# K and Q of the first three pairs of heads, issued by SP and ScalarE instead of SP alone

## The chip, the cores and the metric

One core of one Trainium2 chip. The metric is device time in microseconds (us); the kernel before took 608.39 us in the median of three runs. Engines: TensorE (PE; PEld is its weight load), VectorE (DVE), ScalarE (ACT), GpSimd (POOL) and SyncE (SP), which here only issues transfers.

## What is computed

Attention over 4 sequences of 576 tokens with 8 heads of 64, masked in blocks of 64, then two expert layers on the 2304 tokens. Cut to what matters:

```python
scores = (q @ k.T) / 8                     # per head; masked where block_i < block_j
x = softmax(scores) @ v                    # heads side by side: (2304, 512)
x = maximum(maximum(x @ w1, x @ w2), x @ w3) @ w_out
# then a layer of 8 experts: rows with x @ w_skip > 0 get the arg-max expert of x @ w_gate:
#   x + gate * (relu(x @ w1[e]) @ w2[e])
```

## The kernel before

The tokens are worked in six chunks of 384 (`CH`). For each chunk, attention runs by pairs of heads: a group is one chunk's tokens of one sequence and one pair (`groups`, L564 to L568). Chunk 0 has four groups, one for each pair, all of sequence 0. A group has units of up to 128 queries (`units`, L593 to L596); each of the first four groups has three, with 128, 256 and 384 keys.

`load(i)` (L571 to L582) brings a group's K and Q. The two heads of a pair lie on partitions 0 to 63 and 64 to 127 of the tiles `k` and `q`, and each half is a transfer of its own: K and Q of the first head, then K and Q of the second, four issues on SP, 96 KB each in chunk 0. `load_v` (L584) brings V. `load_ident` (L963) brings the identity that the transposes need. The weights of the first expert layer come as 18 pieces of 512 KB (`raw_words`, L492) and 6 of its second matrix; each is decoded on ScalarE and VectorE (L503 to L534).

A unit of attention is a chain over engines: scores on TensorE (L613, then a mask product at L620), a maximum on VectorE (L637) and its scaling (L651), the exponentials on ScalarE (L662), sums and reciprocals on VectorE (L673, L677), normalizing on either (L683, L685), transposes on TensorE (L697), a copy out (L702), the product with V (L716), and two parts of the result (L726, L724). When all units of a chunk are done, the dense products with the decoded weights (L742) start for it.

`start_masks` (L953) writes the masks on VectorE and runs one small exponential on ScalarE (L961), in front of which ScalarE loads its table.

**The order of the work.** The order on every engine is made when the program is built, by a planner (`Plan`, L60). `build` (L158) makes one `Task` for each step with an engine, a planned duration, a due time `at`, the tasks it depends on and the buffers it takes. `order` (L94) draws tasks one by one: on each engine those that can start within 0.05 planned us of the earliest compete, the lowest due time wins, and of the five engines' winners the earliest start is taken (of equal starts, the engine that comes first in PE, ACT, DVE, POOL, SP). The tasks are then sorted by planned start and emitted, so each engine's queue runs in that order. A task with `nbytes` ends when a planned transfer has ended (one after another, at 230 GB/s) and 2.0 planned us have gone by.

A load of K and Q is a task on SP of 2.5 planned us (L188), the identity one of 0.6 (L182), V one of 0.5 (L193), a weight piece one of 0.6 (L292), the constants one of 1.8 (L287). There are three buffers for Q, six for K, two for V and three for weight pieces (L1026). A Q buffer is free again when all scores of its group are done (L279), so the fourth group's load waits for the first group's scores. Scores depend on their group's load:

```python
deps.append(kq[i])                                                              # L212
sc = S.add("PE", dur, at, lambda ks=ks: [E.sc(k) for k in ks], deps, acq, mode="R")
```

Of the kernel before, what the change touches and what calls it, by code (L numbers as in the profile page):

```python
# [8 lines left out]
F32 = mybir.dt.float32  # L9
# [8 lines left out]
B, H, S, D = 4, 8, 576, 64  # L18
# [3 lines left out]
P = 128  # L22
CH = 384
# [126 lines left out]
def act_time(n, src="psum"):  # L150
    return (0.04 if src == "psum" else 0.09) + 0.83e-3 * n


def dve_time(n, fast=False):
    return 0.07 + (0.52e-3 if fast else 1.045e-3) * n


def build(S, E, groups, units):  # L158
# [4 lines left out]
    def later(name, t, *readers):  # L163
        for r in readers:
            r.releases.append((name, t))

    kq, vv = {}, {}
# [5 lines left out]
    for u in units:  # L173
        c = u[1]
        n = seen.get(c, 0)
# [4 lines left out]
        first_of.setdefault(u[0], k)  # L180
    start = S.add("DVE", 1.0, -1e3, E.masks)
    ident = S.add("SP", 0.6, when[0] - 11.5, E.ident, nbytes=65536)  # L182
    sc_of, pv_of, k_tile = {}, {}, {}
    for i, (c, b, qlo, qhi, tiles, hp) in enumerate(groups):
        at = when[first_of[i]] - 12
        names = ["q"] + (["k"] if qlo == 0 else [])
        n = qhi - qlo
        t = kq[i] = S.add("SP", 2.5, at, lambda i=i: E.load(i), acq=names, nbytes=2 * P * n * 4)  # L188
        if qlo == 0:
            k_tile[b, hp] = t  # L190
        else:
            t.deps.append(k_tile[b, hp])
        vv[i] = S.add("SP", 0.5, at + 1, lambda i=i: E.load_v(i), acq=["v"], nbytes=(qhi + P - 1) // P * P * P * 4)  # L193
# [3 lines left out]
    n = 0  # L197
# [7 lines left out]
    for ks in su:  # L205
        at = when[ks[0]]
        dur, acq, deps = 0.0, [], [start]
        for k in ks:
            i, c, hp, q0, nq, nk, col, first = units[k]
            dur += nk * 4 / 2400 + 0.05  # L210
            acq += ["sc"] * (2 if nk > 512 and nq == P else 1)
            deps.append(kq[i])  # L212
        sc = S.add("PE", dur, at, lambda ks=ks: [E.sc(k) for k in ks], deps, acq, mode="R")
        tps = []
        for n, k in enumerate(ks):
            i, c, hp, q0, nq, nk, col, first = units[k]
            at = when[k]
            nkt = (nk + P - 1) // P
            sets, parts = (1, 2 if nk > 512 else 1) if nq == 64 else (2, 2 if nk > 512 else 1)
            w = nk // parts  # L220
            one = dve_time(w * 2 if sets == 2 else w * parts)
            mk = [S.add("DVE", 0.13, at - 2.2, lambda k=k: E.mk(k), [sc])] if nq == P and c > 1 else []
            mx = S.add("DVE", one * (parts if sets == 2 else 1), at - 2, lambda k=k: E.mx(k), [sc] + mk)
            if parts == 2:
                mx = S.add("DVE", 0.07, at - 2.5, lambda k=k: E.m2(k), [mx])
            mx = S.add("DVE", 0.07, at - 2.5, lambda k=k: E.ms(k), [mx])
            exs = []
            for j in range(sets):
                exs.append(S.add("ACT", parts * (0.24 + 0.83e-3 * w), at - 2 + 0.1 * j, lambda k=k, j=j: E.ex(k, j),
                                 [mx] + exs, ["p"] if j == 0 else []))  # L230
            for _ in range(2 if nk > 512 and nq == P else 1):
                later("sc", sc, *exs)
            rs = S.add("DVE", 0.07, at - 3, lambda k=k: E.ra(k), exs)
            rs = S.add("DVE", 0.08, at - 3, lambda k=k: E.rs(k), [rs])
            nms = []
            for j in range(sets):
                nm = S.add(dict(ACT=0.19 + 0.83e-3 * nk, **(dict(DVE=0.13 + 0.52e-3 * nk) if c != 1 else {})), 0, at - 2.5 + 0.1 * j, None, [rs])
                nm.emit = lambda k=k, j=j, nm=nm: E.nm(k, j, nm.on)
                nms.append(nm)
            todo = sets * nkt  # L240
            evs = []
            for m in range(0, todo, 4):
                z = min(4, todo - m)
                tp = S.add("PE", 0.107 * z, at - 1, lambda k=k, m=m: E.tp(k, m),
                           nms + [ident] + ([tp0] if m else []),
                           ["tp"] + (["pT"] if m == 0 else []), mode="T")
                ev = S.add(dict(ACT=act_time(128 * z), **(dict(DVE=dve_time(128 * z)) if c > 1 else {})), 0, at - 5, None, [tp])
                ev.emit = lambda k=k, m=m, ev=ev: E.ev(k, m, ev.on)
                later("tp", tp, ev)
                later("p", exs[0], tp)  # L250
                if m == 0:
                    tp0 = tp
                evs.append(ev)
            last_pv[k] = (tp0, evs, nkt)
        deps, dur, acq = [], 0.0, []
        for k in ks:
            i, c, hp, q0, nq, nk, col, first = units[k]
            deps += last_pv[k][1] + [vv[i]]
            dur += last_pv[k][2] * (0.213 if nq == P else 0.107)
            acq.append("tp")  # L260
        c = units[ks[0]][1]
        if c not in x_first:
            acq.append("x")
        pv = S.add("PE", dur, when[ks[0]] - 0.5, lambda ks=ks: [E.pv(k) for k in ks], deps, acq, mode="C")
        x_first.setdefault(c, pv)
        if pv is not x_first[c]:
            pv.deps.append(x_first[c])
        for k in ks:
            i, c, hp, q0, nq, nk, col, first = units[k]
            xh = S.add("ACT", act_time(nq), when[k] - 4, lambda k=k: E.xh(k), [pv])  # L270
            xl = S.add("DVE", dve_time(nq), when[k] - 4, lambda k=k: E.xl(k), [xh])
            later("tp", pv, xl)
            later("pT", last_pv[k][0], pv)
            all_x[c] += [xh, xl]
            sc_of.setdefault(units[k][0], []).append(sc)
            pv_of.setdefault(units[k][0], []).append(pv)
# [13 lines left out]
    for k in range(18 + NF):  # L290
        at = first_w + w_pace * k if k < 18 else 16 + 3.0 * (k - 18)
# [22 lines left out]
    for c in range(NCH):  # L314
# [3 lines left out]
        for f in range(NF):  # L318
            for i in range(3):
                at = base + (3 * f + i) * 2.1  # L320
                deps = piece[3 * f + i] + all_x[c] + (prev_y if f == i == 0 else [])
# [21 lines left out]
        at = base + 38  # L343
# [39 lines left out]
    for q in range(8):  # L383
        deps = [go] if q < 3 else [free] if q == 3 else split[q - 4]
        raw = S.add("SP", 0.6, base - 20 + 4 * q, lambda q=q: E.expert_raw(q), deps, nbytes=1 << 20)
        if q < 6:
# [4 lines left out]
            for i in range(2):  # L391
                at = base + 4 * q + 2 * i
# [5 lines left out]
def kernel(  # L398
# [43 lines left out]
    wr_sb = const.tile([P, ND, NG], F32, name="wr_sb")  # L442

    _moe1_phase(tc, nc, const, small, locals())


def _moe1_phase(tc, nc, const, small, g):
# [5 lines left out]
    wr_sb, x2, table, out, counts = (g[n] for n in ("wr_sb", "x2", "table", "out", "counts"))  # L453
# [3 lines left out]
    def open_pool(stack, **kw):  # L457
        return stack.enter_context(tc.tile_pool(**kw))

    with ExitStack() as st_y:  # L460
# [8 lines left out]
        kvp = open_pool(st_a, name="kvp", bufs=2, side="right")  # L469
# [16 lines left out]
        k_all = [None] * NHP  # L486
# [81 lines left out]
                    groups.append((c, b, qlo, qhi, tiles, hp))  # L568
        gdat = [dict() for _ in groups]

        def load(i):  # L571
            c, b, qlo, qhi, tiles, hp = groups[i]
            gd = gdat[i]
            if qlo == 0:
                k_all[hp] = kvp.tile([P, S], F32, tag="k", name="k", bufs=6)
            gd["k"] = k_all[hp]
            gd["q"] = kvp.tile([P, CH], F32, tag="q", name="q", bufs=3)
            for j in range(2):
                src = kq0[hp, 0:64] if b == 0 else kqT[b - 1, hp, 64 * j:64 * j + 64]
                rows = slice(64 * j, 64 * j + 64)  # L580
                nc.sync.dma_start(out=gd["k"][rows, qlo:qhi], in_=src[:, j, qlo:qhi])
                nc.sync.dma_start(out=gd["q"][rows, 0:qhi - qlo], in_=src[:, 2 + j, qlo:qhi])  # L582

        def load_v(i):  # L584
            c, b, qlo, qhi, tiles, hp = groups[i]
# [133 lines left out]
        def s_out(k, lo):  # L719
# [5 lines left out]
            else:  # L725
                nc.scalar.copy(xh, pv)  # L726

        E.load, E.load_v, E.sc, E.mx, E.ex, E.ra, E.rs = load, load_v, s_scores, s_max, s_exp, s_sum, s_recip
        E.m2, E.ms, E.nm, E.mk = s_max2, s_max_scale, s_norm, s_mask
        E.tp, E.ev, E.pv = s_trans, s_turned, s_pv  # L730
# [294 lines left out]

        work = Plan(dict(sc=2, tp=2, mo=2, p=3, pT=2, raw=3, dec=2, hm=4, y=2, k=6, q=3, v=2, x=2))  # L1026
        build(work, E, groups, units)
        with tc.manual_schedule():
            for t in work.order():
# [576 lines left out]
```

## Time and profile before

| | us |
|---|---|
| median of three runs | 608.39 (607.75 to 609.62) |
| the profiled execution, its own time | 606.07 |
| span of its profile | 604.3 |
| TensorE busy in the span | 580.9 |

The profile shows one execution. A row of an order in time gives the start and the length in us, the engine, the line of the kernel, the operation, the tile written and the tile read, and in brackets how long the engine stood idle before it and what released it. `SPq` is SP's own queue: its rows are the issues of transfers, and the data lands later. ScalarE's busy time does not count issues.

### The profile page before, as it was taken

The page shows a single profiled execution, that of the slowest core. Times are in us where ns is not written, and L with a number is a line of the kernel's source. Part 1 is how long each engine was busy: PE and PEld are TensorE (multiplying, and loading weights), DVE is VectorE, ACT ScalarE, POOL GpSimd, SP SyncE. Part 2 cuts the span into 40 slices and gives each one's busy share as a digit, 9 for nine tenths or more (in the row PEclk, how much of TensorE's full clock was granted, in tenths as well). Part 3 has the DMA queues.
Part 4 walks back from the last instruction along what each step waited for, and adds up shares of the span by engine and source line. Part 5 has one row for each costly group of instructions (what it writes and reads, how often), then busy time and mean ns, then how long its engine had stood idle before and what let it go on. Part 6 is the DMA issues. An engine that isn't in the chain of part 4 may idle for free. (4 is left out here: it accounts for less than half of the span.)

```text
span 604.3 us, 11723 instructions
## 1 busy us (share of the span) xinstructions
PE 580.9 (96%) x4250; PEld 493.8 (82%) x4250; DVE 358.2 (59%) x1072; ACT 310.6 (51%) x819; POOL 44.2 (7%) x101
## 2 busy tenths in 40 slices
PE   6889999999999999999999999999999999999994
PEld 3558798699888998888978889988899997788742
DVE  4899999925556435656256553665643775368600
ACT  4899768942666415545235444266642451158420
POOL 1000000002000001000100000200000202311101
PEclk9999999999999999999999999999999999999998
DMA  6564655521111130102212222100006741799980
GB/s 182 162 182 150 205 158 157 148 94 47 44 35 35 51 115 24 40 15 67 105 40 56 61 79 93 56 29 23 2 18 220 277 166 36 213 371 389 355 290 23
DMA packets 61095, 72.73 MB, mean 120 GB/s; under 512 B 7571, under 2 KB 40597, under 8 KB 61024
## 3 DMA queue, kind: packets, MB, share of 16 engines
q1 hardware_dynamic: 59424, 68.88, 35.5%
q0 software_dynamic: 1600, 2.96, 1.5%
q8 instruction: 38, 0.62, 0.5%
q14 instruction: 33, 0.27, 0.1%
HBM read 61.13 MB, written 11.04 MB: 119 GB/s over the span
## 5 line engine op out<-in xcount | busy, mean ns | idle before, releaser
L742 PE MATMUL ps_h<-x,w 128*128 128x384 f32 x1296 | 244.6, 341 | 0.5 <-DVE hm L751 0.5
L742 PEld LDWEIGHTS ps_h<-x,w 128*128 128x128 f32 x1296 | 222.5, 188 | 8.2 <-issue 6.0
L662 ACT ACTIVATE p<-sc,nm 128x288 f32<-128x288 f32 (+7 forms) x168 | 85.1, 515 | 45.7 <-DVE nm L651 44.0
L613 PE MATMUL sc<-k,q 64*64 64x288 f32 (+9 forms) x384 | 66.5, 450 | 6.6 <-DMA q<-in_kq_dram 5.0
L702 ACT COPY pT<-tp 128x512 f32<-128x512 f32 (+2 forms) x98 | 47.9, 505 | 46.6 <-PE tp L697 45.9
L697 PE MATMUL tp<-cst_sb,p 128*128 128x128 f32 x432 | 65.2, 282 | 4.2 <-ACT pT L702 1.8
L793 PE MATMUL ps_y<-wo,h_h 128*128 128x256 f32 (+1 forms) x360 | 68.9, 287 | 0.0
L697 PEld LDWEIGHTS tp<-cst_sb,p 128*128 128x128 f32 x432 | 49.5, 143 | 20.0 <-issue 9.1
L716 PE MATMUL pv<-pT,vt 128*64 128x128 f32 (+1 forms) x960 | 60.4, 270 | 1.6 <-ACT pT L702 1.5
L716 PEld LDWEIGHTS pv<-pT,vt 128*64 128x64 f32 x960 | 48.0, 138 | 14.0 <-issue 6.0
L793 PEld LDWEIGHTS ps_y<-wo,h_h 128*128 128x128 f32 x360 | 56.7, 189 | 1.2 <-issue 1.2
L637 DVE TENSOR_REDUCE nm<-sc 128x2 f32<-128x256 f32 (+7 forms) x64 | 49.2, 786 | 8.6 <-PE sc L620 8.6
L613 PEld LDWEIGHTS sc<-k,q 64*128 64x128 f32 (+1 forms) x384 | 30.6, 180 | 25.6 <-issue 10.3
L793 PE MATMUL ps_y<-wo,h_l 128*128 128x256 f32 (+1 forms) x180 | 51.2, 284 | 0.0
L683 ACT ACTIVATE p<-p,r 128x128 f32<-128x128 f32 (+8 forms) x77 | 44.1, 593 | 8.4 <-DVE r L677 7.8
L751 DVE TENSOR_TENSOR hm<-ps_h,ha 128x384 f32<-128x384 f32 x36 | 20.0, 556 | 28.2 <-PE ps_h L742 24.5
L662 ACT ACTIVATION_READ_ACCUMULATOR p<-sc,nm 128x1 f32 x168 | 34.8, 207 | 0.0
L793 PEld LDWEIGHTS ps_y<-wo,h_l 128*128 128x128 f32 x180 | 34.0, 189 | 0.0
L755 ACT CAST h_h<-hm 128x384 fp32r<-128x384 f32 x36 | 18.5, 515 | 29.8 <-DVE hm L751 29.7
L726 ACT CAST x<-pv 128x128 fp32r<-128x128 f32 (+1 forms) x80 | 19.7, 262 | 26.4 <-PE pv L716 26.2
L659 POOL MEMSET p<- 128x128 f32 (+1 forms) x48 | 9.3, 202 | 319.7 <-PE tp L697 206.5
L751 DVE TENSOR_TENSOR hm<-ps_h,hm 128x384 f32<-128x384 f32 x36 | 20.0, 555 | 21.1 <-PE ps_h L742 20.7
(221 smaller groups left out, 688.8 us busy)
## 6 DMA issues: line engine op xcount, KB each, us to landing
raw<-in_m_w_dram SPq DMA_DIRECT2D x19, 1024.0 KB, 7.6
raw<-in_w_dram SPq DMA_DIRECT2D x18, 512.0 KB, 4.2
vt<-in_v_dram SPq DMA_DIRECT2D x16, 320.0 KB, 3.2
x<-y SPq DMA_DIRECT2D x18, 256.0 KB, 2.1
out_dram<-y SPq DMA_DIRECT2D x18, 256.0 KB, 2.4
xa<-in_m_w_dram SPq DMA_DIRECT2D x4, 1024.0 KB, 8.3
xb<-in_m_w_dram SPq DMA_DIRECT2D x4, 1024.0 KB, 8.0
raw<-in_w_out_dram SPq DMA_DIRECT2D x6, 512.0 KB, 3.6
```

The lines of the kernel that those rows point to most:

```text
L613: nc.tensor.matmul(bank[:, 0:hi - lo], gd["q"][rows, q0:q0 + nq], gd["k"][rows, lo:hi], start=True, stop=packed or hi != nk or c > 1)
L637: nc.vector.tensor_reduce(nm, first_ps[:, :, 0:w], axis=AX.X, op=ALU.max, negate=True)
L662: nc.scalar.activation(u["p"][:, j, lo:hi], src, AF.Exp, bias=u["nm"][:, j:j + 1], scale=0.125, accum_out=u["su"][:, n, j:j + 1])
L683: nc.scalar.activation(pt, pt, AF.Copy, scale=r)
L697: nc.tensor.transpose(tp[:, n, :], u["p"][:, j, t * P:(t + 1) * P], ident)
L702: copy(u["pT"][:, m:m + z], u["tp", m][:, 0:z])
L716: nc.tensor.matmul(pv[64 * j:64 * j + 64, 0:nq], vt[:, t, 64 * j:64 * j + 64], pT, start=(t == 0), stop=(t == nkt - 1))
L726: nc.scalar.copy(xh, pv)
L742: nc.tensor.matmul(ps, a[:, d, :], x[:, d, :], start=(n == 0), stop=(n == 3 * ND - 1))
L751: nc.vector.tensor_tensor(nxt, hm_at["ps", i], hm_at[f], op=ALU.max)
L755: nc.scalar.copy(hid[0][:, f, :], hm_at[f])
L793: nc.tensor.matmul(ps, a[:, f, hs], x[:, f, lo:hi], start=(n == 0), stop=(n == 3 * NF - 1))
```

## The change

For the first three groups (`i < 3`: the first three pairs of heads of chunk 0) the load is split in two tasks: SP issues K and Q of the first head, ScalarE issues K and Q of the second. Each has a planned length of 1.25 us and half the bytes. The ScalarE task takes no buffers and depends on nothing; the scores of these groups depend on both. All other loads stay as they were. `load` gets the halves to load and the engine's issue function as arguments, and takes its tiles once for both tasks.

```diff
--- before.py
+++ after.py
@@ -180,12 +180,16 @@
         first_of.setdefault(u[0], k)
     start = S.add("DVE", 1.0, -1e3, E.masks)
     ident = S.add("SP", 0.6, when[0] - 11.5, E.ident, nbytes=65536)
-    sc_of, pv_of, k_tile = {}, {}, {}
+    sc_of, pv_of, k_tile, other = {}, {}, {}, {}
     for i, (c, b, qlo, qhi, tiles, hp) in enumerate(groups):
         at = when[first_of[i]] - 12
         names = ["q"] + (["k"] if qlo == 0 else [])
         n = qhi - qlo
-        t = kq[i] = S.add("SP", 2.5, at, lambda i=i: E.load(i), acq=names, nbytes=2 * P * n * 4)
+        if i < 3:
+            t = kq[i] = S.add("SP", 1.25, at, lambda i=i: E.load_0(i), acq=names, nbytes=P * n * 4)
+            other[i] = [S.add("ACT", 1.25, at, lambda i=i: E.load_1(i), nbytes=P * n * 4)]
+        else:
+            t = kq[i] = S.add("SP", 2.5, at, lambda i=i: E.load(i), acq=names, nbytes=2 * P * n * 4)
         if qlo == 0:
             k_tile[b, hp] = t
         else:
@@ -209,7 +213,7 @@
             i, c, hp, q0, nq, nk, col, first = units[k]
             dur += nk * 4 / 2400 + 0.05
             acq += ["sc"] * (2 if nk > 512 and nq == P else 1)
-            deps.append(kq[i])
+            deps += [kq[i]] + other.get(i, [])
         sc = S.add("PE", dur, at, lambda ks=ks: [E.sc(k) for k in ks], deps, acq, mode="R")
         tps = []
         for n, k in enumerate(ks):
@@ -568,18 +572,19 @@
                     groups.append((c, b, qlo, qhi, tiles, hp))
         gdat = [dict() for _ in groups]
 
-        def load(i):
+        def load(i, halves=(0, 1), dma=nc.sync.dma_start):
             c, b, qlo, qhi, tiles, hp = groups[i]
             gd = gdat[i]
-            if qlo == 0:
-                k_all[hp] = kvp.tile([P, S], F32, tag="k", name="k", bufs=6)
-            gd["k"] = k_all[hp]
-            gd["q"] = kvp.tile([P, CH], F32, tag="q", name="q", bufs=3)
-            for j in range(2):
+            if "q" not in gd:
+                if qlo == 0:
+                    k_all[hp] = kvp.tile([P, S], F32, tag="k", name="k", bufs=6)
+                gd["k"] = k_all[hp]
+                gd["q"] = kvp.tile([P, CH], F32, tag="q", name="q", bufs=3)
+            for j in halves:
                 src = kq0[hp, 0:64] if b == 0 else kqT[b - 1, hp, 64 * j:64 * j + 64]
                 rows = slice(64 * j, 64 * j + 64)
-                nc.sync.dma_start(out=gd["k"][rows, qlo:qhi], in_=src[:, j, qlo:qhi])
-                nc.sync.dma_start(out=gd["q"][rows, 0:qhi - qlo], in_=src[:, 2 + j, qlo:qhi])
+                dma(out=gd["k"][rows, qlo:qhi], in_=src[:, j, qlo:qhi])
+                dma(out=gd["q"][rows, 0:qhi - qlo], in_=src[:, 2 + j, qlo:qhi])
 
         def load_v(i):
             c, b, qlo, qhi, tiles, hp = groups[i]
@@ -725,6 +730,7 @@
             else:
                 nc.scalar.copy(xh, pv)
 
+        E.load_0, E.load_1 = lambda i: load(i, (0,)), lambda i: load(i, (1,), nc.scalar.dma_start)
         E.load, E.load_v, E.sc, E.mx, E.ex, E.ra, E.rs = load, load_v, s_scores, s_max, s_exp, s_sum, s_recip
         E.m2, E.ms, E.nm, E.mk = s_max2, s_max_scale, s_norm, s_mask
         E.tp, E.ev, E.pv = s_trans, s_turned, s_pv
```

## Rows read from the trace of the kernel before

**Rows 1.** The page: each engine's busy us, share of the span, instructions
```profile
PE 580.9 (96%) x4250; PEld 493.8 (82%) x4250; DVE 358.2 (59%) x1072; ACT 310.6 (51%) x819; POOL 44.2 (7%) x101
```

**Rows 2.** Stages: length, busy us of PE, PEld, DVE, ACT, POOL; clock, DMA, GB/s
```profile
0.00:8.00 8.00, 2.65 (x12) 1.75 (x12) 1.52 (x10) 2.16 (x6) 1.87 (x13) 1.00 0.55 146
...
8.00:20.00 12.00, 11.46 (x72) 6.81 (x72) 8.40 (x33) 8.20 (x30) 0.00 (x0) 1.00 0.84 235
...
20.00:40.00 20.00, 15.59 (x135) 9.35 (x135) 19.42 (x63) 19.78 (x65) 0.15 (x1) 1.00 0.52 148
...
40.00:100.00 60.00, 59.97 (x454) 51.96 (x456) 59.31 (x147) 48.87 (x114) 1.10 (x5) 1.00 0.57 173
...
100.00:122.00 22.00, 19.70 (x193) 15.31 (x189) 19.98 (x68) 19.25 (x63) 1.71 (x8) 1.00 0.47 136
...
122.00:560.00 438.00, 435.80 (x3210) 387.26 (x3210) 239.35 (x745) 203.24 (x533) 35.22 (x70) 1.00 0.30 97
```

**Rows 3.** Order in time, PE: a later unit's scores, the first dense products
```profile
26.66 0.56 PE L613 MATMUL sc<-k,q 64*128 64x128 f32 x4 [0.22 <-ACT p L662]
...
42.11 4.43 PE L742 MATMUL ps_h<-x,w 128*128 128x384 f32 x24
```

**Rows 4.** Order in time, PE: the first scores and transposes
```profile
3.99 0.76 PE L613 MATMUL sc<-k,q 64*128 64x128 f32 x2 [3.99 <-DMA q<-in_kq_dram]
...
5.73 0.55 PE L613 MATMUL sc<-k,q 64*128 64x128 f32 x1 [0.98 <-DMA q<-in_kq_dram]
...
8.19 1.65 PE L613 MATMUL sc<-k,q 64*128 64x384 f32 x4 [0.57 <-ACT p L662]
...
9.82 0.69 PE L697 MATMUL tp<-cst_sb,p 128*128 128x128 f32 x2
...
10.44 0.80 PE L613 MATMUL sc<-k,q 64*128 64x128 f32 x4
```

**Rows 5.** Order in time, SP's queue: the first loads
```profile
0.74 0.59 SPq L581 DMA_DIRECT2D k<-in_kq_dram  x1
...
1.39 0.58 SPq L582 DMA_DIRECT2D q<-in_kq_dram  x1
...
2.65 0.60 SPq L582 DMA_DIRECT2D q<-in_kq_dram  x1
...
3.28 0.59 SPq L964 DMA_DIRECT2D cst_sb<-in_cst_dram  x1
...
3.91 0.43 SPq L589 DMA_DIRECT2D vt<-in_v_dram  x1
...
9.93 0.59 SPq L496 DMA_DIRECT2D raw<-in_w_dram  x1
```

**Rows 6.** DMA issues of 0-2, 2-3.3, 0-30 us: KB, us to landing
```profile
q<-in_kq_dram SPq DMA_DIRECT2D x1, 96.0 KB, 2.5
...
q<-in_kq_dram SPq DMA_DIRECT2D x1, 96.0 KB, 3.0
...
raw<-in_w_dram SPq DMA_DIRECT2D x4, 512.0 KB, 4.6
```

**Rows 7.** Order in time, VectorE: the first maximum
```profile
6.60 0.42 DVE L637 TENSOR_REDUCE nm<-sc 128x2 f32<-128x256 f32 x1 [5.03 <-PE sc L620]
```

**Rows 8.** Order in time, ScalarE: up to the first exponential
```profile
0.75 1.28 ACT L961 ACT_TABLE_LOAD   x1 [0.75 <-PEq L1593]
...
2.04 0.20 ACT L961 ACTIVATE warm<-warm 128x2 f32<-128x2 f32 x1
...
7.33 0.37 ACT L662 ACTIVATE p<-sc,nm 128x128 f32<-128x128 f32 x1 [5.08 <-DVE nm L651]
```

**Rows 9.** Order in time, GpSimd: its one early issue of a transfer
```profile
1.80 0.75 POOL L979 DMA_DIRECT2D table<-dummy  x1
```

**Rows 10.** Order in time, ScalarE: the first decode step
```profile
18.78 0.68 ACT L505 ACTIVATE dec<-raw 128x512 f32<-128x512 f32 x1
```

**Rows 11.** Waits of TensorE from 40 us on: us, times, longest
```profile
PE pv L716 <- ACT pT L702: 1.5, 3, 0.8
```

## The prediction, made before the change was run

> **What bounds the kernel now.** I read the page's busy table first, then the span cut into stages, then each engine's order of instructions in the first microseconds, then who TensorE waited for. The page says TensorE is busy 580.9 of 604.3 us [rows 1], so the end is TensorE's work plus its gaps, and a change pays only what it takes out of a gap. The stages say where the gaps are [rows 2]: up to 40 us TensorE is busy 2.65 + 11.46 + 15.59 = 29.70 us and idle 10.30; from 40 to 100 us it misses 0.03 us in all; from 100 to 122 us it misses 2.30; over the next 438 us it misses 2.20. So the opening is where something can be won. Its end is the first dense product of the expert layer at 42.11 us [rows 3], which needs the whole first chunk of attention; from there TensorE runs closed.
>
> Inside the opening there are two regimes. Up to 20 us no engine is full: between 8 and 20 us VectorE is busy 8.40 of 12 us and ScalarE 8.20, so a chain of short dependent steps sets the pace. From 20 to 40 us VectorE is busy 19.42 and ScalarE 19.78 of 20 [rows 2]: they are full, with weights to decode beside attention.
>
> The chain begins with loads. The first scores wait until 3.99 us for the first head's K and Q; the second head's score product stands from 4.75 to 5.73 us for its own Q [rows 4]. SP issued these four from 0.74 to 2.65 us, one every 0.64 us [rows 5], and the last landed 3.0 us after its issue [rows 6], at 5.65. VectorE's first maximum follows at 6.60 and ScalarE's first exponential at 7.33, after 5.08 us idle [rows 7, 8].
>
> **The change part by part.**
> The second head's loads. ScalarE's queue is free from 0.75 us [rows 8]. In the planner the new ScalarE task has no inputs and no buffers to wait for, so it is drawn at planned time 0, ahead of the warm-up: K and Q of the second head leave at about 0.75 and 1.39 us, not 2.01 and 2.65, 1.26 earlier. They land between 1.39 + 2.5 = 3.89 and 1.39 + 3.0 = 4.39 [rows 6]. TensorE can take the second head when the first is done, at 4.75, so it gains 5.73 - 4.75 = 0.98 us. If the two pairs slow each other so that both land near 4.3, the first head starts 0.3 late and the gain is 0.7. I take 1.0: the DMA engines were 0.55 busy over the first 8 us [rows 2], so there is room for two pairs at once.
>
> ScalarE's new work. No row shows an issue on ScalarE. From below: SP's shortest in this stretch is 0.43 us, from above: GpSimd's 0.75 [rows 5, 9]; nearest are SP's own issues of the same K and Q at 0.59, a step of 0.64 with the gap, which I take. Six make 3.84 us. With the table load and the warm-up (1.28 + 0.20, [rows 8]) they fill ScalarE from 0.75 to 6.1. The first exponential is due at 7.33 - 1.0 = 6.3. So they lie in ScalarE's idle 5.08 us and cost nothing, but barely: at a step of 0.68 they end just at 6.3, at 0.85 the whole gain is gone, at 0.80 (GpSimd's issue and a gap) 0.3 us of it is left. A step of 0.48 gives nothing more. Behind these issues in ScalarE's queue stand the exponentials, and behind them VectorE and TensorE.
>
> SP's queue. It loses six issues, 6 x 0.64 = 3.84 us, in front of the first weight piece. The identity goes from 3.28 to about 2.0, V of the first pair from 3.91 to 2.6, the first weight piece from 9.93 to 6.1 [rows 5]. The identity is first read at 9.82 and V after that [rows 4], so nothing comes of these. The second pair's scores start at 10.44 with no load to wait for [rows 4]: no gain there beyond the shift.
>
> The planner books 1.25 us on SP instead of 2.5 for these three loads, so by its own figures SP is through with them at 3 x 1.25 + 1.6 = 5.35 instead of 3 x 2.5 + 1.6 = 9.1, the 1.6 being the identity and two V. The fourth pair's load cannot go then: it needs a Q buffer, freed by the first pair's last scores (8.19 plus 1.65 us in the trace, [rows 4]). So all three weight pieces and the constants should now go ahead of it, where one piece did [rows 5]. It is read only by the tenth unit of scores, at 26.66 us [rows 3]. Three pieces of 0.52 MB at the 235 GB/s of 8 to 20 us [rows 2] take 6.7 us, so it lands by some 18 us: hidden.
>
> Weights earlier. The first decode step starts at 18.78 us [rows 10]; its piece will be there 3.8 us sooner. That can fill VectorE's 3.6 idle us of 8 to 20. But the dense start at 42.11 asks for the first chunk's attention, and decode steps set between its steps delay them too. I count nothing for this in the forecast; between nothing and the 2.3 us TensorE misses from 100 to 122 us, where VectorE and ScalarE are again full (19.98 and 19.25 of 22), it goes into a rival.
>
> Sum: -1.0 at the start, 0 for ScalarE, 0 for the rest. From 20 to 40 us the full engines get their work 1.0 earlier and pass it 1.0 earlier; after 42 us TensorE's work is unchanged. The profiled execution took 606.07 us (span 604.3 and 1.8 around it), so 605.1; its median stands 2.3 higher, 608.39, so **607.4**.
>
> **The rivals.**
> A. The weights help too. The start gives 1.0, and decoding ahead takes out some or all of the 2.3 us of 100 to 122 us, or as much of the 4.41 us that TensorE misses from 20 to 40. 605.1 to 606.5. For it: both stretches have VectorE and ScalarE full; against it: attention waits in the same queues.
>
> B. The issues delay each other, and the exponentials stand behind them: slower. If SP's and ScalarE's issues go through one descriptor generator in turn, each step doubles to 1.28 us. ScalarE then has 0.75 + 2 x 1.28 + 1.48 + 4 x 1.28 = 9.9 us before its first exponential, 2.6 later than 7.33, and the second head's Q leaves no sooner than before. 611.0. It decides against the change from a step of 0.85 us on, and passes 0.3% from 1.16. Against it: SP issued a 0.52 MB weight piece in the same 0.59 us as a 0.10 MB K [rows 5, 6], so an issue's time does not grow with its bytes, and more data in flight need not lengthen it; for it: no row shows two such queues at once.
> The Trainium skill has this rule (Perfetto Trace Analysis, DMA Instruction — HWDGE (DVE, Sync)): the generator is one block, locked by one sequencer at a time, and an issue's profiled time includes the wait for that lock. If the lock is held for the whole 0.59 us, B follows; no run so far shows it.
>
> C. The halves share the transfers and nothing lands earlier: both pairs come when the last came, 5.65 us, and the time stays at 608.4. Against it: three or more 0.10 MB loads were under way at once with landing times of 2.5 to 3.0 us [rows 6], so four cost little more.
> The Trainium skill says so (DMA: Bandwidth & Descriptors, Rules for kernel authors): two transfers to the two partition halves serialize on the same 16 engines. The landing times speak against it at this size.
>
> D. The planner draws another order. Its new task lengths move every later choice, and one more wait of 0.8 us per chunk over the first four, the longest that TensorE has for a ScalarE copy after 40 us [rows 11], makes 3.2 us, less the 1.0: 610.6.
>
> **How the numbers follow.** A measurement here can tell 0.3%, 1.8 us, from no change. Forecast (607.4): 0.42, within it. A: 0.30, faster. C: 0.08, the same. B: 0.12 and D: 0.08, slower. So faster 0.30, same 0.50, slower 0.20. The range reaches below A by the 0.7 us by which the runs shown differ from their median (607.75 to 609.62): 604.4; above it takes in D and what of B has a step up to 1.2 us: 610.8. Left out: the worse half of B and a few in a hundred at each end. The forecast's own range, 0.3 to 1.0 us gained and that spread, is 606.7 to 608.8.
>
> **What would show it.** Right: the second head's scores right behind the first's near 4.8 us, the first maximum near 5.6, ScalarE's issues of some 0.6 us over before 6.3, the first exponential there, the first weight piece issued near 6.1, the dense start near 41. Wrong: issues of 1.2 us on either queue (B); the first scores later than 4.4 us (C); an early exponential but a dense start at 42 or later (the gain lost between decode steps, or D); a dense start before 40, or no gap from 100 to 122 us (A).

## The result, and the profile after

The changed kernel takes 610.91 us (median of 16 runs, 608.23 to 613.58) against 607.63 for the kernel before (16 runs on the same chip, 605.27 to 609.62): ratio 1.0059, interval 1.0045 to 1.0074. It is slower, by twice what a measurement here can tell, and just outside the range. The profiled execution has a span of 609.7 us, 5.4 over that of before.

The page of the kernel after: TensorE's row and the clock granted to it, in 40 equal slices of 15.2 us; the last line is the clock's row of the page before.

```profile
span 609.7 us, 11718 instructions
...
PE 583.6 (96%) x4250; PEld 494.7 (81%) x4250; DVE 356.7 (59%) x1074; ACT 312.3 (51%) x817; POOL 44.1 (7%) x101
...
PEclk9999999799999999999999999999999999999998
...
PEclk9999999999999999999999999999999999999998
```

The 7 in the eighth slice is the result in one digit. The stages, cut as in [rows 2], put a number to it:

```profile
0.00:8.00 8.00, 2.06 (x14) 1.56 (x14) 1.75 (x10) 2.29 (x6) 1.87 (x13) 1.00 0.68 185
...
40.00:100.00 60.00, 59.33 (x468) 51.22 (x466) 59.09 (x145) 50.39 (x119) 1.47 (x7) 1.00 0.58 175
100.00:122.00 22.00, 21.05 (x165) 17.88 (x165) 17.82 (x67) 17.66 (x56) 0.71 (x4) 0.85 0.42 125
122.00:560.00 438.00, 433.15 (x3193) 383.62 (x3193) 236.06 (x742) 200.36 (x528) 35.74 (x72) 1.00 0.30 95
```

Where before had 2.30 us of gaps from 100 to 122 us at clock 1.00, after has 0.95 of gaps at 0.85. A TensorE that looks fuller is running slower. In slices of two microseconds:

```profile
112.00:114.00 2.00, 1.34 (x14) 1.03 (x12) 2.00 (x8) 1.75 (x8) 0.20 (x1) 1.00 0.58 162
114.00:116.00 2.00, 1.85 (x17) 1.19 (x16) 1.97 (x10) 1.18 (x4) 0.00 (x0) 0.88 0.04 10
116.00:118.00 2.00, 1.92 (x10) 1.76 (x10) 0.99 (x4) 1.92 (x8) 0.00 (x0) 0.50 0.38 101
118.00:120.00 2.00, 2.00 (x14) 1.64 (x14) 0.63 (x4) 1.00 (x6) 0.00 (x0) 0.50 0.17 51
120.00:122.00 2.00, 2.00 (x11) 2.00 (x11) 0.36 (x2) 1.20 (x4) 0.00 (x0) 0.50 0.36 109
122.00:124.00 2.00, 2.00 (x19) 1.80 (x18) 0.08 (x1) 0.49 (x2) 0.00 (x0) 0.91 0.18 55
```

0.50 is the lower of TensorE's two levels, 1.2 of 2.4 GHz; in the trace it is granted from 115.5 us for 6.8 us. TensorE's order there shows what it did before it fell and what the fall does to one and the same instruction:

```profile
109.96 1.06 PE L553 MATMUL psw<-wr_sb,wt 128*128 128x10 f32 x8
110.95 0.66 PE L721 MATMUL pv<-pT,vt 128*64 128x128 f32 x8
...
113.23 1.06 PE L553 MATMUL psw<-wr_sb,wt 128*128 128x10 f32 x8 [0.66 <-ACT wt L548]
114.22 0.34 PE L721 MATMUL pv<-pT,vt 128*64 128x64 f32 x4
...
116.99 1.79 PE L553 MATMUL psw<-wr_sb,wt 128*128 128x10 f32 x8
118.70 1.12 PE L721 MATMUL pv<-pT,vt 128*64 128x128 f32 x8
```

Eight products of w_out with the router's 10 columns take 1.06 us at full clock and 1.79 at half; eight products with V take 1.12 where they took 0.66 at 110.95. Before the fall TensorE stood 0.66 us waiting for a turned block and went through small products only.

The opening, ScalarE's queue (start, us, then the idle time ahead and what ended it):

```profile
0.75 0.56 ACTq L586 DMA_DIRECT2D k<-in_kq_dram  x1
1.34 0.61 ACTq L587 DMA_DIRECT2D q<-in_kq_dram  x1
1.98 1.28 ACT L967 ACT_TABLE_LOAD   x1 [1.98 <-issue]
2.04 0.55 ACTq L586 DMA_DIRECT2D k<-in_kq_dram  x1
2.62 0.62 ACTq L587 DMA_DIRECT2D q<-in_kq_dram  x1
3.27 0.20 ACT L967 ACTIVATE warm<-warm 128x2 f32<-128x2 f32 x1
3.28 0.66 ACTq L586 DMA_DIRECT2D k<-in_kq_dram  x1
4.83 0.47 ACTq L587 DMA_DIRECT2D q<-in_kq_dram  x1
7.10 0.37 ACT L667 ACTIVATE p<-sc,nm 128x128 f32<-128x128 f32 x1 [3.62 <-DMA k<-in_kq_dram]
```

and TensorE's first scores and first dense product:

```profile
5.37 0.90 PE L618 MATMUL sc<-k,q 64*128 64x128 f32 x4 [5.37 <-DMA q<-in_kq_dram]
...
41.86 4.43 PE L748 MATMUL ps_h<-x,w 128*128 128x384 f32 x24
```

Both heads' scores now start together, at 5.37; before, the first started at 3.99 and the second stood until 5.73 [rows 4]. In this profile the first exponential comes 0.23 us earlier than before [rows 8] and the dense start 0.25 us earlier [rows 3]. The second profiles of both kernels, from runs told below, say how much that is worth. Their first exponentials, the kernel before first and the changed kernel behind it:

```profile
7.03 0.37 ACT L662 ACTIVATE p<-sc,nm 128x128 f32<-128x128 f32 x1 [4.78 <-DVE nm L651]
...
7.33 0.37 ACT L667 ACTIVATE p<-sc,nm 128x128 f32<-128x128 f32 x1 [3.83 <-DMA k<-in_kq_dram]
```

So 7.33 and 7.03 before, 7.10 and 7.33 after: no gain is shown. The second head's scores start at 5.73 and 5.43 before, at 5.37 and 5.74 after; in the second profile of the changed kernel the first head's start at 4.19, as they did before.

TensorE's waits from 40 us on (total, times, longest), against [rows 11]:

```profile
PE psa L1256 <- DVE T L1229: 1.3, 1, 1.3
PE pst L1220 <- ACT h L1244: 0.9, 1, 0.9
PE psy L1256 <- issue: 0.8, 1, 0.8
PE tp L702 <- POOL p L664: 0.8, 1, 0.8
PE psa L1333 <- DMA raw<-in_m_w_dram: 0.7, 1, 0.7
PE psw L553 <- ACT wt L548: 0.7, 1, 0.7
```

The attention's waits for ScalarE's copies (1.5 us before) are not among the largest any more, so the new order did not add the wait of rival D. The first line stood before as well (`psa L1250 <- DVE T L1223`, 1.2 us). New are three in the last layer, on pst, psy and psa L1333, 2.4 us together.

Three marks divide each profiled execution: TensorE's first dense product of the first expert layer, its first product of the last layer (psa), and its last product. Before: 42.1, 519.9, 595.7. After: 41.9, 522.0, 601.4. So -0.2 us up to the dense start, +2.3 from there to the last layer, +3.6 in the last layer, by marks rounded to 0.1 us. Together that is 5.7 us at TensorE's last product, of which 0.3 is made up behind it. The experiments take these stretches one by one.

### The profile page after: what moved, and what is told of

Read it like the earlier page. It is cut to its first block, busy times and chain, and to the rows that moved or that the text cites. A ratio compares the mean times of both kernels' runs of the same rounds, so it can differ in the third digit from the quotient of the medians.

```text
span 609.7 us, 11718 instructions
## 1 busy us (share of the span) xinstructions
PE 583.6 (96%) x4250; PEld 494.7 (81%) x4250; DVE 356.7 (59%) x1074; ACT 312.3 (51%) x817; POOL 44.1 (7%) x101
## 5 line engine op out<-in xcount | busy, mean ns | idle before, releaser
L667 ACT ACTIVATE p<-sc,nm 128x288 f32<-128x288 f32 (+7 forms) x168 | 84.6, 513 | 41.4 <-DVE nm L656 36.0
L702 PE MATMUL tp<-cst_sb,p 128*128 128x128 f32 x432 | 66.5, 283 | 4.2 <-DVE p L690 1.1
L799 PE MATMUL ps_y<-wo,h_h 128*128 128x256 f32 (+1 forms) x360 | 70.3, 291 | 0.0
L688 ACT ACTIVATE p<-p,r 128x576 f32<-128x576 f32 (+8 forms) x75 | 43.4, 592 | 10.1 <-DVE r L682 9.2
L806 ACT COPY y<-ps_y 128x256 f32<-128x256 f32 x30 | 11.2, 373 | 42.3 <-PE ps_y L799 42.3
L707 DVE COPY pT<-tp 128x512 f32<-128x512 f32 (+2 forms) x38 | 21.0, 552 | 19.7 <-PE tp L702 19.5
```

The costliest lines, as they stand in the source:

```text
L667: nc.scalar.activation(u["p"][:, j, lo:hi], src, AF.Exp, bias=u["nm"][:, j:j + 1], scale=0.125, accum_out=u["su"][:, n, j:j + 1])
L688: nc.scalar.activation(pt, pt, AF.Copy, scale=r)
L702: nc.tensor.transpose(tp[:, n, :], u["p"][:, j, t * P:(t + 1) * P], ident)
L707: copy(u["pT"][:, m:m + z], u["tp", m][:, 0:z])
L799: nc.tensor.matmul(ps, a[:, f, hs], x[:, f, lo:hi], start=(n == 0), stop=(n == 3 * NF - 1))
```

## The experiments

Theory O: the changed bookings make the planner write another order, and this order costs. Rival Q: the second queue costs. Theory C, formed on the first answers: what the order costs is TensorE's clock. Kernels of one group ran on one chip, with their own runs of before; a ratio given here is not exactly the quotient of the two medians shown.

**First group** (before on its chip: 605.48, 23 runs). The changed order without the second queue:

```
-        E.load_0, E.load_1 = lambda i: load(i, (0,)), lambda i: load(i, (1,), nc.scalar.dma_start)
+        E.load_0, E.load_1 = lambda i: load(i, (0,)), lambda i: load(i, (1,))
```

> The planned order of the changed kernel, but SP issues the second heads as well, in the places where ScalarE did; everything computed as before. Theory O (the new order of the work on the engines costs the time, by a TensorE clock that falls to 0.50 between 115.5 and 122.4 us and by waits of the last layer): still slower than before, 610 to 612 us, with a stretch of clock 0.50 near 115 to 123 us. Theory Q (two queues asking at once cost the time, by transfers that share the engines and issues that wait for each other): back to 607 to 608 us, clock 1.00 up to 600 us.

610.04, ratio 1.0064 (1.0044 to 1.0084): a loss of the same size without a single issue on ScalarE. Its parts are others: its clock falls for longer, 10.2 us from 116.5 on, and for 3.4 us at 41.4, just ahead of the dense start, as well (0.97 from 40 to 100 us), while its last layer is as short as before. The later fall:

```profile
112.00:116.00 4.00, 3.32 (x33) 2.83 (x32) 3.97 (x13) 3.64 (x11) 0.36 (x2) 1.00 0.45 131
116.00:120.00 4.00, 4.00 (x25) 3.33 (x25) 3.08 (x13) 2.88 (x8) 0.00 (x0) 0.57 0.17 49
120.00:124.00 4.00, 4.00 (x23) 3.64 (x24) 1.00 (x6) 2.60 (x10) 0.00 (x0) 0.50 0.21 64
124.00:128.00 4.00, 4.00 (x26) 3.66 (x26) 0.23 (x1) 1.06 (x3) 0.00 (x0) 0.65 0.17 51
```

The second queue without the changed order, from the kernel before: the planner keeps its bookings, SP issues the first heads of three pairs, ScalarE the second heads, ahead of the first planned task and right after it.

```
-            t = kq[i] = S.add("SP", 2.5, at, lambda i=i: E.load(i), acq=names, nbytes=2 * P * n * 4)
+            t = kq[i] = S.add("SP", 2.5, at, lambda i=i: E.load(i, (0,) if i < 3 else (0, 1)), acq=names, nbytes=2 * P * n * 4)
...
+        early = [lambda i=i: load(i, (1,), nc.scalar.dma_start) for i in range(3)]
```

> The planned order of the kernel before, with K and Q of the second heads of the first three pairs issued by ScalarE, in the same places of its queue as in the changed kernel; everything computed as before. Theory O: 607 to 608 us or a little under, no fall of the clock before 600 us; the first scores near 5.4 us as in the changed kernel, the first exponential near 7.1. Theory Q: 610 to 612 us.

605.59, ratio 1.0001 (0.9992 to 1.0010): nothing. From 100 to 122 us TensorE is busy 19.70 us at clock 1.00, as before. The first scores are at 5.22, the first exponential at 6.95. Theory O holds, rival Q falls: the queue by itself costs nothing, the order by itself costs as much as the change.

The same for the first pair alone (3 becomes 1):

> The planned order of the kernel before, with only the first pair's second head issued by ScalarE. If the first scores were late in the changed kernel (5.37 us against 3.99) because the later pairs' transfers were in flight beside the first pair's, the first scores start between 4.0 and 4.5 us and the second head's follow at once; the first exponential at 6.2 to 6.6 us; time 606.6 to 607.4 us. If two queues slow each other whatever they carry, the first scores stay near 5.4 us.

605.71, ratio 0.9995 (0.9982 to 1.0009). This is the step that I had costed, without the four other loads in its way. Its first scores:

```profile
4.83 0.90 PE L614 MATMUL sc<-k,q 64*128 64x128 f32 x4 [4.83 <-DMA q<-in_kq_dram]
```

and its DMA issues of the first 1.5 us (KB each, median us from issue to landing):

```profile
k<-in_kq_dram SPq DMA_DIRECT2D x1, 96.0 KB, 2.8
k<-in_kq_dram ACTq DMA_DIRECT2D x1, 96.0 KB, 2.4
q<-in_kq_dram ACTq DMA_DIRECT2D x1, 96.0 KB, 2.5
q<-in_kq_dram SPq DMA_DIRECT2D x1, 96.0 KB, 3.3
```

The second head's Q is there at 1.34 + 2.5 = 3.84, as forecast; the first head's, issued as before, lands after 3.3 us instead of 2.5 [rows 6], at about 4.7. Of these 0.8 us, 0.26 lie in the issue itself, which takes 0.84 instead of 0.58. The two heads' loads slow each other, and the slower one decides; my range for the first scores, 4.0 to 4.5, was missed. The first exponential comes at 6.56, and the profile's dense start is 40.9, 1.2 us earlier; the runs don't tell it from nothing.

The kernel before once more, for a second profile:

> The kernel before once more, for a second profile of it: all theories expect the milestones of the first profile within 0.3 us up to the last dense products at 500 us, clock 1.00 up to 600 us, and a last layer that shows how far its length varies by itself.

605.89; marks 42.0, 519.9 and 596.0; no fall before the end. The clock of before is no chance of one profile, and none of its 23 runs has a mean clock under 0.993, where the 16 of the changed kernel have 0.986 to 0.991.

**Second group** (before: 607.22, 27 runs). Theory C asks for a kernel with the changed order and no fall. The six products with the router's columns get 60 columns, of which 10 are used:

```
-                nc.tensor.matmul(ps, wt_at[k][:, d, :], wr_sb[:, d, :], start=(d == 0), stop=(d == ND - 1))
+                nc.tensor.matmul(ps, wt_at[k][:, d, :], wr_pad[:, d * NG:(d + 6) * NG], start=(d == 0), stop=(d == ND - 1))
```

> The changed kernel with one edit: the six small products of w_out with the router's columns (L553, eight matmuls of 10 columns each, 1.06 us for eight) take 60 columns instead of 10, 50 of them not used, so that TensorE streams more in the stretch in which the clock fell, at next to no time. Theory C (the loss is the fall of TensorE's clock to 0.50 at about 115 us, and the fall comes of how little these small products stream): the clock stays 1.00 from 104 to 124 us or falls for less, the first dense product of the second chunk's second half (y) starts 2 to 3 us before the 207.2 of the changed kernel, and the time is 0.3 to 0.6% under that of the changed kernel, level with before (604.5 to 607.5). Rival W (the new order itself is worse, the clock is beside the point): the clock may change, but the time stays 0.4 to 0.8% above before. Rival N (what the small products stream is not what decides): the clock still falls at 110 to 120 us, time as the changed kernel.

608.62, ratio 1.0018 (1.0006 to 1.0030). Eight products take 1.10 us instead of 1.06:

```profile
111.57 1.10 PE L557 MATMUL psw<-wr_sb,wt 128*128 128x60 f32 x8 [0.62 <-ACT wt L551]
```

and the stages show that the clock stays up:

```profile
112.00:116.00 4.00, 3.65 (x32) 2.68 (x30) 3.31 (x14) 2.94 (x11) 0.00 (x0) 1.00 0.24 70
116.00:120.00 4.00, 4.00 (x40) 3.57 (x38) 1.20 (x7) 2.79 (x11) 0.00 (x0) 1.00 0.37 109
120.00:124.00 4.00, 4.00 (x37) 3.68 (x36) 0.57 (x3) 1.23 (x3) 0.00 (x0) 1.00 0.08 28
```

The wait for the turned block is still there, 0.62 us; the small products but for their width, the order and the queues are the same. None of its eleven runs has a clock under 0.994. From the dense start to the last layer it takes 477.6 us, after 480.1, before 477.8. So up to the last layer the order by itself costs nothing, and the clock all. The median is still 0.18% above before, clear of the noise, and over the range that I had given for theory C (604.5 to 607.5); in the profile what is left stands in the last layer.

Another way to the same end: TensorE turns the identity four times more ahead of each of the last four of these products.

```
+            if k >= 20:
+                for d in range(4):
+                    nc.tensor.transpose(ps[:, P:2 * P], ident, ident)
```

> The changed kernel with one edit: ahead of the last four of the six small products of w_out (L553) TensorE turns the identity four times more into unused columns of the same PSUM tile: 4 x 0.66 us of added work that needs nothing and so runs where the engine stood waiting for the copied block (0.66 us at 112.57), 1.5 to 2.5 us of it in full. Theory C: the clock stays 1.00 from 104 to 124 us; the 3.4 us lost to the half clock come back and about 2 us of added work are paid: time 0.1 to 0.4% under the changed kernel. Rival W (the order itself): 2 us slower than the changed kernel, 0.3% above it, whatever the clock does. Rival N: the clock falls as before and the added work comes on top, +0.3%.

608.11, ratio 1.0016 (0.9999 to 1.0032): no fall, 478.2 us to the last layer with up to 2.6 us of useless work in it. More work, and 5 us less time than the changed kernel on the same chip, which follows.

The changed kernel beside them:

> The changed kernel once more, beside the three others on one chip. Theory C: the clock falls to 0.50 between 110 and 120 us for several us again, mean clock 0.985 to 0.991, time 0.4 to 0.8% above before. Rival (a single chance of the one profiled execution): no fall in this profile, mean clock 0.997, and the time still 0.4 to 0.8% above before. Whether the last layer's 79.4 us (75.8 before) come again is open: 75.5 to 76.5 if it was chance.

613.16 (5 runs), ratio 1.0089 (1.0056 to 1.0122). The clock falls again, 0.85 from 100 to 122 us, and dense start to last layer is 480.2 us. Its last layer took 78.0 us. Against it the wide products give back 4.5 of the 5.9 us that it takes over before on this chip.

A third order, by other due times of w_out's pieces:

```
-        at = first_w + w_pace * k if k < 18 else 16 + 3.0 * (k - 18)
+        at = first_w + w_pace * k if k < 18 else 20 + 3.5 * (k - 18)
```

> The changed kernel with one edit: the due times of w_out's six pieces go from 16 + 3.0 per piece to 20 + 3.5, so that the planner writes a third order, in which the last dense product of the first half stands later (102.3 of the planner's own scale against 97.4) and which it holds to be 1.0 us shorter than the changed kernel's. Theory C: the time follows the clock: if the clock does not fall between 100 and 124 us, time at or under before (604 to 606.5); if it falls, time 0.3 to 0.9% above before, about 0.5 us for each us at 0.50. Rival W (the two queues' start is what costs): slower than before by 0.4 to 0.8% whatever the order.

609.14, from 604.97 to 613.39, ratio 1.0017 (0.9990 to 1.0044): no verdict on the median, but the spread is strong evidence for C. Three of its eleven runs have a mean clock of 0.996 to 0.997 and spans of 603.2 to 603.7 us; five have 0.983 to 0.985 and 607.3 to 611.6; the other three have 0.990 to 0.993 and 605.8 to 608.1. One program, one chip: its times go with the clock, though not one for one (607.3 at 0.984, 608.1 at 0.990).

**Third group** (before: 607.19, 32 runs). The third order with the wide products:

> The third order (due times 20 + 3.5 per piece) and the wide products (60 columns instead of 10) together, two queues as in the changed kernel. Theory C (the clock alone separates the third order's runs, 603.2 to 603.7 us of span at 0.996 to 0.997 and 607.3 to 611.6 at 0.983 to 0.985): with the wide products no run falls under 0.993, every span is 603 to 606, time 0.2 to 0.4% under before. Rival N (wide products only happened to help one order): runs at 0.983 to 0.985 come again, median as in the third order alone, spread over 603 to 612. Last layer, from its first product to TensorE's last: 78 to 79 us, as in the other kernels with a new order and ScalarE's issues, if these two make it (T); 76.0 to 76.5 if it is chance.

604.84, ratio 0.9965 (0.9947 to 0.9983): faster than both kernels. No run has a clock under 0.994, all spans are 600.5 to 604.8. The stretch in its profile:

```profile
100.00:122.00 22.00, 21.01 (x186) 17.57 (x186) 20.18 (x70) 19.25 (x62) 1.07 (x6) 1.00 0.43 127
```

The remaining three undo the queues: the changed order with wide products and all K and Q from SP, the third order the same, and the third order with ScalarE issuing for the first pair alone.

> The changed kernel's order and the wide products, but all loads of K and Q issued by SP: apart from the queue the same as the run with the wide products alone (608.62, 0.18% above before; last layer 78.7 us). Theory T (the last layer is 2 to 3 us longer only where a new order and ScalarE's six issues come together): last layer 76.0 to 76.5, start 1 us later, time 0.0 to 0.3% under before. Rival (the last layer hangs on the order or on chance): 78 to 79 us here too, time 0.2 to 0.4% above before.

607.22, ratio 1.0012 (0.9996 to 1.0028).

> The third order and the wide products, all loads of K and Q issued by SP: against the same with two queues it shows what the second queue is worth when order and clock are held. Theory: first scores near 5.4 us instead of 5.3, no measurable difference from two queues but for the last layer, 76.0 to 76.5 us (T): time 0.2 to 0.5% under before, at or under the kernel with two queues. Rival (the second queue is worth its 1 us of start once the clock is held): 0.1 to 0.2% above the kernel with two queues.

605.74, ratio 0.9973 (0.9952 to 0.9994).

> The third order and the wide products, and ScalarE issues the second heads of the first pair alone, SP those of the other two pairs. Theory: first scores 4.8 us as where the old order had this, first exponential 6.6, a start 0.5 to 1 us ahead of the kernel with three pairs on two queues, time 0.3 to 0.5% under before. Rival (the start is worth nothing measurable): level with the two others of the third order. Last layer 76.0 to 76.5 if six issues are what makes it longer, 78 to 79 if two are enough.

605.62, ratio 0.9980 (0.9962 to 0.9998). With one order, and no fall from 100 to 130 us in any of the three profiles, one queue, two, or two for one pair give 605.74, 604.84 and 605.62, with intervals that lie over each other: what the second queue itself is worth stays below what these runs can tell. The clock was not held everywhere: the last of the three, and the wide products from SP alone, fall for 3.4 us at 41 us in their profiles, as the new order from SP alone did. My expectation of first scores at 4.8 us for the last one missed: 5.08.

The stretches of all profiles, in us, from TensorE's order in time:

| kernel | order | dense start | to last layer | last layer |
|---|---|---|---|---|
| before, twice | old | 42.1, 42.0 | 477.8, 477.9 | 75.8, 76.1 |
| two queues; first pair alone | old | 41.8, 40.9 | 477.8, 477.8 | 76.1, 76.1 |
| after, twice | new | 41.9, 41.8 | 480.1, 480.2 | 79.4, 78.0 |
| new order, SP alone | new | 43.4 | 481.9 | 76.2 |
| wide products; added turns | new | 40.3, 41.1 | 477.6, 478.2 | 78.7, 78.3 |
| wide products, SP alone | new | 43.1 | 478.2 | 78.1 |
| due times | third | 42.1 | 481.8 | 79.2 |
| due times and wide: two queues, SP alone, first pair | third | 40.9, 41.7, 42.8 | 475.9, 475.9, 476.5 | 78.9, 78.8, 78.5 |

The third column is the clock: 480.1 to 481.9 in the four profiles with a fall between 100 and 130 us, 475.9 to 478.2 in the ten without. The three with a fall at 41 us have the three latest dense starts, 42.8 to 43.4; of that fall 1.3 to 1.5 us lie behind the dense start and cost about 0.7 us there, by which wide products from SP alone (478.2) and the third order with the first pair (476.5) stand above their like (477.6 and 475.9). The start itself scatters: the changed kernel, twice, the wide products and the added turns have one order and the same queues up to there and start at 41.9, 41.8, 40.3 and 41.1. The last column is a second loss that I can't explain. Nine of ten profiles with a new order take 78.0 to 79.4 us for the last layer, the four with the old order 75.8 to 76.1. Some 8 to 10 us into it TensorE stands 1.3 to 1.8 us (in the first profile of the changed kernel in two pieces), in the fastest kernel here:

```profile
PE pst L1225 <- ACT h L1249: 1.3, 1, 1.3
...
PE psa L1338 <- DMA raw<-in_m_w_dram: 0.7, 1, 0.7
```

Theory T, that it takes the new order and ScalarE's issues together, fell with the runs from SP alone (78.1, 78.8). The code of that layer is the same in all. ScalarE, for which TensorE waits there, waits itself for TensorE's signal that the products in `psa` are done: in the second profile of the changed kernel the signal comes 2.2 us behind their end as modelled, in the kernel before and in the exception (76.2) at once. Why it comes late was not found, and the exception says that the order alone does not force it.

## Why the prediction was wrong

The step that failed is in the sum: "0 for the rest", with its reason that "after 42 us TensorE's work is unchanged". The work is unchanged, its place in time is not. I had read the order as free unless it adds waits, and of the clock only that [rows 2] gave 1.00 in every stage. In the new order the last dense products of the first chunk's first half run from 102.0 to 104.4 us where before they were over at 99.5:

```profile
97.10 2.37 PE L742 MATMUL ps_h<-x,w 128*128 128x384 f32 x12
...
102.03 2.37 PE L748 MATMUL ps_h<-x,w 128*128 128x384 f32 x12
```

Behind them come small products only, before for 23.3 us up to 122.8 with the clock kept, after for 11 us until it fell, in both profiles. That the clock is what costs up to the last layer, and that wider products keep it, the runs show; what in the new order makes it fall, where the old one has the longer stretch of small products, they do not. In the profile that is 22 x 0.15 + 2 x 0.09 = 3.5 us of clock time lost, and 2.3 us of time up to the last layer. Rival D named the event, another order, and ended on the right side (610.6, by chance 0.3 us from the measured median); its mechanism, one more wait for a copy per chunk, is not there, and its chance of 0.08 was far too small for an event that the planner's new bookings made certain.

Point by point:

- The start, -1.0: a second step that failed. It measured -0.25 at the dense start, and at the first exponential nothing that two profiles of each kernel show. ScalarE's Q left at 1.34 as forecast, but landed after 3.5 us, and after 4.25 in the second profile, not 2.5 to 3.0. With the first pair alone it landed after 2.5, and the first head's Q 0.8 us later than before; that the loads of the next pairs, put in flight beside it by two queues, cost the rest is argued from this difference. The DMA engines' mean share of 0.55, on which I had relied for room, is a mean over 8 us; it is 0.68 after. Rival C, which I gave 0.08, was half right: in the first profile both heads waited until 5.37, in the second the second head until 5.74, as before. The Trainium skill's rule, that two transfers to the two partition halves serialize on the same engines (DMA: Bandwidth & Descriptors, Rules for kernel authors), points that way; by the landing times of the first pair alone the slowing was 0.8 us of 2.5, not a doubling.
- ScalarE's issues, 0: right. Six of 0.47 to 0.66 us (forecast a step of 0.64), over at 5.30, before 6.1. They ran beside the table load too (the third starts at 2.04, the load lasts to 3.26), which I had added in a row.
- Rival B: no doubling. One of the issues of K and Q on SP took 0.84 us where the same took 0.58 before, the others 0.47 to 0.65 (0.49 to 0.60 before); in the second profile it is one on ScalarE that took 0.80. The Trainium skill's lock (Perfetto Trace Analysis, DMA Instruction — HWDGE (DVE, Sync)) would fit one row in each profile and no more.
- SP's queue: right in kind. Three weight pieces and the constants went ahead of the fourth pair's load, but from 7.95 us on, not 6.1: SP stood 1.7 us in all for landings of earlier loads, for the reason in the last section.
- Rival A: the weights came earlier and the gaps from 100 to 122 us did shrink, from 2.30 to 0.95 us. With the clock kept, the same order has gaps of 0.96 and reaches the last layer in 477.6 us instead of 477.8, so they gave next to nothing by then. The third order with the clock kept shows that there was something to win up to there: 475.9 us.
- The last layer, +2 to 3.6 us in the profiles, stood in no part of the prediction, and its cause stays open.

The sum that would have been right for the first profile: -0.25 for the start, +2.3 for the clock, +3.6 for the last layer, and -0.3 behind TensorE's last product, which make its +5.4. The clock is the smaller part of it. Over the runs, whose clock goes from 0.986 to 0.991, the median difference is 3.3 us; there the clock is the larger part, by the 4.5 of 5.9 us that the wide products gave back.

## What to carry to other kernels

Where a planner orders the work, a changed booking is a changed order everywhere: compare the whole order before and after, and look at TensorE's granted clock in every stretch of small products, not only at its busy share, since a half-clocked engine looks fuller. Here 50 unused columns, for 0.04 us in eight products, held the clock; only with it held can an order be judged. A second queue does not by itself make loads land earlier: with the first pair's second head on it both heads' scores could start at 4.83 us, with three pairs' at 5.37 and, in a second profile, at 5.74, no better than the 5.73 and 5.43 of one queue.

## What was not expected of the hardware

- TensorE busy 3.18 of 4 us from 112 to 116 us was followed by the fall; before had 3.20 of 4 from 116 to 120 and kept 1.00. The busy share does not tell which stretch loses the clock. The same work with wider products lies 1.6 us earlier, is no busier, and kept it:

```profile
110.40:114.40 4.00, 3.10 (x29) 2.21 (x27) 3.96 (x16) 2.94 (x12) 0.20 (x1) 1.00 0.27 82
```

- Both queues pause in the opening, and the pause looks like one of the queue: in the run with the old order and two queues SP's sixth transfer left at 5.10 us and its second, issued at 1.39, landed after 3.7 (5.08); ScalarE's sixth left at 4.92, its second, issued at 1.34, landed after 3.6 (4.90). The trace says that it is one of the program:

```profile
SPq L583 <- DMA q<-in_kq_dram: 0.9, 1, 0.9
```

Each load of the two queues reports its landing on one of eight semaphores, which the program uses in turn, and waits for the landing of the load that had its semaphore last; these two wait for SP's second and for ScalarE's second. No number of transfers in one queue explains it: with the first pair alone on ScalarE, SP's sixth left at 4.05 us while its second landed at 4.69. A second queue uses the eight up sooner; before, where each landing took 2.5 to 3.0 us in a single queue with a step of 0.64, no such pause shows.
